# Rearranging the joins between stages: query groups, guess groups, last heads' values, a row sum in its PSUM copy and a shorter Newton step

## The chip, the core and the metric

The kernel runs on one core of one Trainium2 chip. The time is device microseconds of one execution; lower is better. In the profile PE is TensorE's matmul side, PEld its weight loads, DVE is VectorE, ACT is ScalarE, POOL is GpSimd and SP is SyncE, which here issues nearly all DMAs.

## The reference

Four layers with residuals on a sequence of 2048 tokens of 640 features, in bf16: spectral layer A, memory layer B, A, B.

```python
def _A_ref(x, w_r, w_i):                      # x is layer-normed
    X = rfft2(x.astype(float32)) * (w_r + 1j * w_i)
    return irfft2(X, s=(2048, 640)).astype(bfloat16)

def _B_ref(x, mem0, Wq, Wk, Wv, Wo, seg_len): # 64 segments of 32 tokens, 8 memory rows, 32 heads of 128
    mem = mem0
    for s in range(64):
        h = concat([mem, x[segment s]])
        q, k, v = h @ Wq, h @ Wk, h @ Wv
        p = softmax(where(mask, q @ k.T * 128 ** -0.5, -1e9))
        o = (p @ v) @ Wo
        mem = o[:8]
        out[segment s] = o[8:]

x = x + _A_ref(layernorm(x)); x = x + _B_ref(layernorm(x))
x = x + _A_ref(layernorm(x)); x = x + _B_ref(layernorm(x))
```

## The kernel before

**Layer A** does its Fourier transforms as matmuls against tables. `spectrum` transforms, filters and transforms back along one axis. `tokens` (L567) finishes 16 rows of 128 tokens each: `spectrum_d` and `tokens(s0)` on PE, a PSUM copy of row s0 by ACT into x (L597), then the layer norm of the next layer. The statistics come from DVE (`stats`, L603), only for row 15 from ACT (`act_stats`, L606): an Identity pass with a summed output (L609), a Square pass with a summed output that uses the sum as its bias (L610), and on POOL the mean (L611). `inverse(q)` turns the variance of a pair of rows into a reciprocal square root: Ln and Exp on ACT (L112, L113), then a Newton step in `_ln_inverse`. It has five steps on POOL (L117 to L121) for pairs 0 to 6 and four on DVE (L115, L119 to L121) for the last pair, 7. `norm(q)` scales the pair's rows on DVE (L127) and stores them to `xn`.

Inside the same stage the next layer B is prepared (`BStart`). `add_u` sums the rows of each segment on PE (L1541). `rows_in` and `rows_out` transpose the normed rows into `hT`. `guess1` (L1554) multiplies the segment means by Wv for groups of heads given by `GUESS` (L1552), each group in one PSUM bank, and `guess1_out` (L1567) copies each bank to SBUF, the last group by ACT and the one before by DVE. The result, times Wo (`guess2`, L1627), is a guess of each segment's memory row, so that all 64 segments can run at once; a later check compares it with the true memory rows.

**Layer B** (`_b_fast_pass`, L1080) runs over heads h = 0 to 33. Heads 0 and 1 have their queries in `q_x` before and after the guess: four groups of 15 segments (480 columns), one of 3 (96 columns) and a tail of one segment (28 + 4 columns), each a chain of five matmuls into a PSUM tile that ACT copies out with the scale (L1149, L1138). These tiles, the guess's, those of the key and value chains, and in the end those of the wide sums, share a pool of three banks (`pj`). In step h the dense chains of head h (`dense`: keys, queries, values) are interleaved by `merge` with dependent work of earlier heads (`dep`): scores of head h-1, sums of the softmax, and on odd h the `value_group`s of heads h-3 and h-2. `merge` runs, after dense item i, the dependent steps until n * len(dense) reaches (i + 1) * len(dep); `pause` is an empty step. A value group is four matmuls (two for the last) into one of two `pso` banks (L1277), then a product with the reciprocal sums on DVE (L1291 to L1294), which frees the bank. The reciprocals of heads up to 30 come back from DRAM as a broadcast (`sums_back`, L1261).

At h = 32 there are no dense chains left. First come the scores of head 31 beside output matmuls (`begin` makes a list of seven blocks of four matmuls of the output projection, L1470). Then `wide` holds five sums of head 31 (`sums_wide`: four matmuls, then Ln and Exp on ACT, L1267 to L1270), `fill` seven output blocks, and `groups` the five value groups of head 30. In step 33 the value groups of head 31 are merged with a third list of output blocks. `_FastOut.run` then finishes the output projection, and for the first memory layer normalises each finished block of 128 tokens for the second spectral layer.

The order on PE, ACT and DVE is the order of the calls (`manual_schedule`); inside the head loop SP's is too. Around `tokens`, POOL's and SP's orders are the scheduler's.

Of the kernel before, what the change touches and what calls it, by code (L numbers as in the profile page):

```python
# [10 lines left out]
FP32 = mybir.dt.float32  # L11
BF16 = mybir.dt.bfloat16
I32 = mybir.dt.int32
ALU = mybir.AluOpType
# [5 lines left out]
S, D = 2048, 640  # L20
# [87 lines left out]
def _ln_inverse(nc, pool, mv, nt, eps_t, small):  # L108
# [5 lines left out]
    if small is nc.vector:  # L114
        small.scalar_tensor_tensor(out=t, in0=mv[:, :nt, 1], scalar=LN_EPS, in1=r0, op0=ALU.add, op1=ALU.mult)  # L115
    else:
        small.tensor_scalar_add(out=t, in0=mv[:, :nt, 1], scalar1=LN_EPS)  # L117
        small.tensor_tensor(out=t, in0=t, in1=r0, op=ALU.mult)
# [73 lines left out]
class LayerA:  # L192
# [374 lines left out]
    def tokens(self, x_dst, xn_dst, handoff=None):  # L567
# [16 lines left out]

        def tokens(s0):
# [11 lines left out]
            nc.scalar.copy(out=halves(x[:, s0, :]), in_=psy[:, :, 0:320])  # L597
# [8 lines left out]
        def act_stats(s0):  # L606
            m, scr = mv[s0 // 2][:, s0 % 2, :], Gs[1].rearrange("p a b -> p (a b)")[:, 0:D]
            nm = wk.tile([128, 1], FP32, name="lnnm", tag="lnnm")
            nc.scalar.activation(out=scr, in_=x[:, s0, :], func=ACTF.Identity, scale=-D ** -1.5, accum_out=nm[:])  # L609
            nc.scalar.activation(out=scr, in_=x[:, s0, :], func=ACTF.Square, scale=D ** -0.5, bias=nm[:, 0:1], accum_out=m[:, 1:2])  # L610
            nc.gpsimd.tensor_scalar_mul(out=m[:, 0:1], in0=nm[:], scalar1=-D ** 0.5)  # L611
# [468 lines left out]
def _b_fast_pass(tc, g, bs, env, flag_col, nxt=None):  # L1080
# [29 lines left out]
    if True:  # L1110
# [25 lines left out]
        def q_tail(QT, ps, lo, src0, n):  # L1136
            b = st.qbase(NSEG - 1) + lo
            nc.scalar.mul(out=QT[:, b:b + n], in_=ps[:, src0:src0 + n], mul=scale)  # L1138

        def q_x(w, h):  # L1140
            QT = QTs[h % 2]
            for g_ in range(NG):
# [7 lines left out]
            ps = pj.tile([128, 512], FP32, name="psq", tag="pj")  # L1150
            b = st.kbase(NSEG - 1) + 1
            chain(w["Wq"], h % 2, ps[:, 0:SEG - st.TAIL], hT, b, b + SEG - st.TAIL)
            chain(w["Wq"], h % 2, ps[:, SEG - st.TAIL:SEG], hT, st.TAILK, st.TAILK + st.TAIL)
            q_tail(QT, ps, 0, 0, SEG)
# [182 lines left out]
        if True:  # L1337
            for h in range(H + 2):
# [39 lines left out]
                if h < H:  # L1378
# [4 lines left out]
                    else:  # L1383
# [7 lines left out]
                        else:  # L1391
                            dep = [pause]
# [7 lines left out]
                elif h == H:  # L1400
# [13 lines left out]
                    for i, f in enumerate(wide):  # L1414
                        f()
                        for _ in range(2):
                            (fill or groups).pop(0)()
                    groups.pop(0)()
# [94 lines left out]
class BStart:  # L1513
# [38 lines left out]
    GUESS = ((0, 8), (8, 16), (16, 24), (24, 28), (28, 32))  # L1552
# [246 lines left out]
```

## Time and profile before

| | |
|---|---|
| median of 4 runs | 1563.13 us (1562.32 to 1564.14) |
| profiled execution | 1564.03 us, of which span 1562.2 us |
| PE busy | 1532.5 us, 98% of the span, 14482 matmuls |
| DVE, ACT, POOL busy | 809.5, 772.9, 234.8 us |
| granted TensorE clock | 0.999 |

Busy times are summed over the span. A row of the timeline is start, duration, engine, line, operation, tiles and count, and in brackets the idle time just before it and what ended it. The two pairs of layers are alike: the join from A to B is at 104 to 124 us and again at 872 to 892, the end of the last head at 612 to 656 and at 1378 to 1422. Matmul ends are modelled: two matmuls of one stream overlap in the records, and a pause is read best from one matmul's start to the next one's.

### The profile page before, as it was taken

Reading aid. Unit: us, or ns where it says so; the run is one execution under the profiler, and the core shown is the slowest. Engines: PE = TensorE matmul, PEld = TensorE weight load, DVE = VectorE, ACT = ScalarE, POOL = GpSimd, SP = SyncE. Lnnn points to the kernel's source line nnn. Section 1 sums busy time; section 2 is a strip of 40 time slices with the busy share of each in tenths; the row PEclk is TensorE's granted clock in tenths of the full one; section 3 lists DMA queues with packets and bytes.
Section 4 is the critical chain, followed back from the end, with each engine's and each line's share of the span. In section 5 each row is a group of like instructions: output and inputs, shape, how many; then the busy total and the mean of one; then the engine's idle time right before and its main releaser. Section 6 shows DMA issues by size and latency. Waiting matters only on the chain. (4 is left out here: it accounts for less than half of the span.)

```text
span 1562.2 us, 36535 instructions
## 1 busy us (share of the span) xinstructions
PE 1532.5 (98%) x14482; PEld 1077.6 (69%) x14483; DVE 809.5 (52%) x2432; ACT 772.9 (49%) x2251; POOL 234.8 (15%) x327
## 2 busy tenths in 40 slices
PE   7999999999999999999999999999999999999998
PEld 6776666666666666677777766666666666667775
DVE  7873545555456555633367535565455545553111
ACT  4583565556555565511136655556555565562000
POOL 3520121111111121100034101112111121110000
PEclk9999999999999999999999999999999999999999
DMA  4780344334433444646114514344434434327242
GB/s 171 227 298 28 110 142 148 136 126 147 152 138 137 146 127 149 193 107 183 51 48 159 182 49 144 137 138 134 166 126 139 151 122 174 124 99 230 70 128 64
DMA packets 159765, 214.87 MB, mean 138 GB/s; under 512 B 7136, under 2 KB 133096, under 8 KB 151648
## 3 DMA queue, kind: packets, MB, share of 16 engines
q1 hardware_dynamic: 159008, 210.14, 41.0%
q8 instruction: 115, 1.88, 0.5%
q0 software_dynamic: 576, 2.30, 0.4%
q14 instruction: 66, 0.54, 0.1%
HBM read 167.32 MB, written 45.10 MB: 136 GB/s over the span
## 5 line engine op out<-in xcount | busy, mean ns | idle before, releaser
L1128 PEld LDWEIGHTS <-bB_S 128*128 128x128 bf16 x3180 | 261.2, 97 | 179.8 <-issue 0.6
L1187 DVE CAST bB_S<-psk 128x495 bf16<-128x495 f32 (+3 forms) x320 | 191.6, 599 | 277.3 <-PE psk L1128 272.6
L1470 PE MATMUL psx<-Wo_sb,bB_S 128*128 128x320 bf16 x2048 | 287.7, 299 | 0.1
L1207 ACT ACTIVATE bB_S<-pss 128x269 bf16<-128x269 f32 (+5 forms) x576 | 208.8, 386 | 139.0 <-PE pss L1204 138.7
L1470 PEld LDWEIGHTS <-bB_S 128*128 128x128 bf16 x2048 | 197.1, 98 | 74.4 <-DVE bB_S L1291 0.7
L1172 ACT ACTIVATE bB_S<-psq 128x96 bf16<-128x96 f32 x300 | 152.4, 508 | 173.4 <-PE psq L1128 173.4
L1247 POOL TENSOR_TENSOR bB_S<-bB_S,bB_S 128x535 f32<-128x535 f32 x90 | 111.7, 1254 | 821.1 <-DVE bB_S L1239 763.1
L1291 DVE TENSOR_TENSOR bB_S<-pso,bB_S 128x480 bf16<-128x480 f32 (+1 forms) x320 | 192.8, 603 | 78.9 <-DMA bB_S<-Rd 50.4
L1208 DVE TENSOR_TENSOR bB_S<-bB_S,maskf 128x269 bf16<-128x269 bf16 (+5 forms) x576 | 159.0, 289 | 109.2 <-ACT bB_S L1207 109.2
L1196 ACT CAST bB_S<-psv 128x512 bf16<-128x512 f32 (+1 forms) x288 | 162.7, 565 | 80.9 <-PE psv L1194 80.9
L1194 PE MATMUL psv<-bB_S,B2hT_S 128*128 128x256 bf16 x1360 | 168.8, 272 | 0.0
L1194 PE MATMUL psv<-bB_S,B1hT_S 128*128 128x256 bf16 x1360 | 168.7, 272 | 0.0
L1128 PE MATMUL psk<-B2hT_S,bB_S 128*128 128x495 bf16 (+3 forms) x800 | 164.2, 343 | 0.2 <-ACT bB_S L1149 0.2
L1128 PE MATMUL psk<-B1hT_S,bB_S 128*128 128x495 bf16 (+3 forms) x800 | 164.2, 343 | 0.2 <-ACT bB_S L1149 0.2
L1128 PE MATMUL psq<-B2hT_S,bB_S 128*128 128x495 bf16 (+5 forms) x780 | 156.0, 336 | 0.0
L1128 PE MATMUL psq<-B1hT_S,bB_S 128*128 128x495 bf16 (+5 forms) x780 | 155.9, 336 | 0.0
L1194 PEld LDWEIGHTS <-B1hT_S 128*128 128x128 bf16 x1360 | 129.8, 98 | 24.4
L1194 PEld LDWEIGHTS <-B2hT_S 128*128 128x128 bf16 x1360 | 129.8, 98 | 24.4
L1204 PE MATMUL pss<-bB_S 128*128 128x132 bf16 (+8 forms) x1152 | 137.5, 219 | 0.0
L1204 PEld LDWEIGHTS <-bB_S 128*128 128x128 bf16 x1152 | 95.5, 97 | 55.3
L1277 PE MATMUL pso<-bB_S,bB_S 128*128 128x132 bf16 (+8 forms) x1152 | 118.5, 219 | 3.5 <-DVE oTmf L1294 2.8
L1277 PEld LDWEIGHTS <-bB_S 128*128 128x128 bf16 x1152 | 89.1, 98 | 36.3 <-DVE oTmf L1294 4.6
(293 smaller groups left out, 1427.0 us busy)
## 6 DMA issues: line engine op xcount, KB each, us to landing
bB_S<-Rd SPq DMA_DIRECT2D x62, 1070.0 KB
oTx_d<-bB_S SPq DMA_DIRECT2D x60, 512.0 KB
bB_S<-oTx_d SPq DMA_DIRECT2D x46, 512.0 KB
bB_S<-in_B_Wq_dram SPq DMA_DIRECT2D x32, 320.0 KB
bB_S<-in_B_Wk_dram SPq DMA_DIRECT2D x32, 320.0 KB
bB_S<-in_B_Wv_dram SPq DMA_DIRECT2D x32, 320.0 KB
Wo_sb<-in_B_Wo_dram SPq DMA_DIRECT2D x4, 1280.0 KB
B1wv_S<-in_B_Wv_dram SPq DMA_DIRECT2D x10, 512.0 KB
```

The source lines that it names most:

```text
L1128: nc.tensor.matmul(ps, lhsT=w[:, ch, hh * 128:(hh + 1) * 128], rhs=src[:, ch, lo:hi], start=(ch == 0), stop=(ch == 4))
L1172: nc.scalar.mul(out=qv[:, :, 0:SEG], in_=x_view(ps, o, n)[:, :, 1:SW], mul=scale)
L1187: nc.vector.tensor_copy(out=KTs[h % 2][:, lo:hi], in_=ps[:, 0:hi - lo])
L1194: nc.tensor.matmul(ps[:, i * 256:(i + 1) * 256], lhsT=hT[:, ch, st.hcol((t + i) * 128):st.hcol((t + i) * 128) + 128], rhs=w["Wv"][:, ch, : ...
L1196: nc.scalar.copy(out=V[:, t:t + n, :].rearrange("p a b -> p (a b)"), in_=ps[:, 0:n * 256])
L1204: nc.tensor.matmul(ps[:, off - o0:off - o0 + hi - lo], lhsT=KT[:, t * 128:(t + 1) * 128], rhs=QT[:, lo:hi], start=True, stop=True)
L1207: nc.scalar.activation(out=E[:, 0:n], in_=ps[:, 0:n], func=ACTF.Exp)
L1208: nc.vector.tensor_tensor(out=P[:, o0:o0 + n], in0=E[:, 0:n], in1=bs.mask[:, o0:o0 + n], op=ALU.mult)
L1247: nc.gpsimd.tensor_tensor(out=acc, in0=acc, in1=part, op=ALU.add)
L1277: nc.tensor.matmul(pso[:, lo - q0:hi - q0], lhsT=V[:, t, (h % 2) * 128:(h % 2 + 1) * 128], rhs=P[:, off:off + hi - lo], start=(i == 0), st ...
L1291: nc.vector.tensor_tensor(out=oT.rearrange("p (r s j) -> p r s j", r=16, j=2)[:, :, s0:s0 + ns, :], in0=byclass(po), in1=rx, op=ALU.mult)
L1470: self.tc.nc.tensor.matmul(ps[:, 0:320], lhsT=lhs(h, k // 2), rhs=self.g["Wo_sb"][:, h, c0:c0 + 320], start=(h == 0), stop=(h == H - 1))
```

## The change

- `_ln_inverse` on DVE has three steps in place of four; POOL's form stays.
- Row 15's copy out of PSUM also gives the row's sum; the Identity pass of `act_stats` becomes a scaling of that sum.
- `q_x` does the tail and the group of three segments first, then the four groups of 15.
- Head 31's list of dependent steps has one more `pause` in front.
- At h = 32, `wide`, the output blocks and the value groups of head 30 alternate in another order: sums group, (from the third on a value group of head 30 ahead of it), one output block; then the fourth value group, the two blocks left over, the sums, and the last group.
- The last two guess groups have 6 and 2 heads in place of 4 and 4.

```diff
--- before.py
+++ after.py
@@ -113,6 +113,9 @@
     nc.scalar.activation(out=r0, in_=r0, func=ACTF.Exp, scale=-0.5)
     if small is nc.vector:
         small.scalar_tensor_tensor(out=t, in0=mv[:, :nt, 1], scalar=LN_EPS, in1=r0, op0=ALU.add, op1=ALU.mult)
+        small.scalar_tensor_tensor(out=t, in0=t, scalar=-0.5, in1=r0, op0=ALU.mult, op1=ALU.mult)
+        small.scalar_tensor_tensor(out=t, in0=t, scalar=1.5, in1=r0, op0=ALU.add, op1=ALU.mult)
+        return rs, nb
     else:
         small.tensor_scalar_add(out=t, in0=mv[:, :nt, 1], scalar1=LN_EPS)
         small.tensor_tensor(out=t, in0=t, in1=r0, op=ALU.mult)
@@ -582,6 +585,8 @@
                     nc.tensor.matmul(psg[:, e, 0:NF], lhsT=UT[0:m, ch, e, s0, :], rhs=Gd[0:m, ch, e, :], start=(ch == 0), stop=(ch == 2))
             nc.scalar.copy(out=Gs[s0 % 3], in_=psg[:, :, 0:NF])
 
+        nm = wk.tile([128, 1], FP32, name="lnnm", tag="lnnm")
+
         def tokens(s0):
             q, t = s0 // 2, s0 % 2
             if t == 0:
@@ -594,7 +599,10 @@
             nc.tensor.matmul(psy[:, 0, 0:320], lhsT=Ti[:, s0, 0, :], rhs=G[:, 1, 0:320], start=False, stop=True)
             nc.tensor.matmul(psy[:, 1, 0:320], lhsT=Ti[:, s0, 0, :], rhs=G[:, 0, 320:0:-1], start=False, stop=False)
             nc.tensor.matmul(psy[:, 1, 0:320], lhsT=Ti[:, s0, 1, :], rhs=G[:, 1, 320:0:-1], start=False, stop=True)
-            nc.scalar.copy(out=halves(x[:, s0, :]), in_=psy[:, :, 0:320])
+            if s0 < 15:
+                nc.scalar.copy(out=halves(x[:, s0, :]), in_=psy[:, :, 0:320])
+            else:
+                nc.scalar.activation(out=halves(x[:, s0, :]), in_=psy[:, :, 0:320], func=ACTF.Identity, accum_out=nm[:])
             if t == 1:
                 nc.sync.dma_start(out=xd[:, 2 * q:2 * q + 2, :], in_=x[:, 2 * q:2 * q + 2, :])
 
@@ -605,8 +613,7 @@
 
         def act_stats(s0):
             m, scr = mv[s0 // 2][:, s0 % 2, :], Gs[1].rearrange("p a b -> p (a b)")[:, 0:D]
-            nm = wk.tile([128, 1], FP32, name="lnnm", tag="lnnm")
-            nc.scalar.activation(out=scr, in_=x[:, s0, :], func=ACTF.Identity, scale=-D ** -1.5, accum_out=nm[:])
+            nc.scalar.mul(out=nm[:], in_=nm[:], mul=-D ** -1.5)
             nc.scalar.activation(out=scr, in_=x[:, s0, :], func=ACTF.Square, scale=D ** -0.5, bias=nm[:, 0:1], accum_out=m[:, 1:2])
             nc.gpsimd.tensor_scalar_mul(out=m[:, 0:1], in0=nm[:], scalar1=-D ** 0.5)
 
@@ -1139,7 +1146,12 @@
 
         def q_x(w, h):
             QT = QTs[h % 2]
-            for g_ in range(NG):
+            ps = pj.tile([128, 512], FP32, name="psq", tag="pj")
+            b = st.kbase(NSEG - 1) + 1
+            chain(w["Wq"], h % 2, ps[:, 0:SEG - st.TAIL], hT, b, b + SEG - st.TAIL)
+            chain(w["Wq"], h % 2, ps[:, SEG - st.TAIL:SEG], hT, st.TAILK, st.TAILK + st.TAIL)
+            q_tail(QT, ps, 0, 0, SEG)
+            for g_ in (NG - 1, 0, 1, 2, 3):
                 n = GS if g_ < NG - 1 else 3
                 b = st.hcol(st.kbase(g_ * GS))
                 ps = pj.tile([128, 512], FP32, name="psq", tag="pj")
@@ -1147,11 +1159,6 @@
                     nc.tensor.matmul(ps[:, 0:n * SEG], lhsT=w["Wq"][:, ch, (h % 2) * 128:(h % 2 + 1) * 128], rhs=x_view(hT[:, ch, :], b, n)[:, :, 1:SW],
                                      start=(ch == 0), stop=(ch == 4))
                 nc.scalar.mul(out=x_view(QT, st.qbase(g_ * GS), n)[:, :, 0:SEG], in_=ps[:, 0:n * SEG].rearrange("p (s t) -> p s t", t=SEG), mul=scale)
-            ps = pj.tile([128, 512], FP32, name="psq", tag="pj")
-            b = st.kbase(NSEG - 1) + 1
-            chain(w["Wq"], h % 2, ps[:, 0:SEG - st.TAIL], hT, b, b + SEG - st.TAIL)
-            chain(w["Wq"], h % 2, ps[:, SEG - st.TAIL:SEG], hT, st.TAILK, st.TAILK + st.TAIL)
-            q_tail(QT, ps, 0, 0, SEG)
 
         def q_m(w, h):
             QT = QTs[h % 2]
@@ -1389,7 +1396,7 @@
                             for f, p in zip(v0[1:] + v1, parts):
                                 dep += [p, f]
                         else:
-                            dep = [pause]
+                            dep = [pause, pause]
                             for f, p in zip(v0, parts):
                                 dep += [f, p]
                             dep += parts[5:] + [pause]
@@ -1411,11 +1418,14 @@
                     load_block(2, ((NT, 24), (24, HL)))
                     wide = [lambda g_=g_: sums_wide(P[h - 1], Rb[h - 1], g_) for g_ in range(NG)]
                     fill = begin()
-                    for i, f in enumerate(wide):
+                    for n in range(NG):
+                        if n > 1:
+                            groups.pop(0)()
+                        wide[n]()
+                        fill.pop(0)()
+                    groups.pop(0)()
+                    for f in fill:
                         f()
-                        for _ in range(2):
-                            (fill or groups).pop(0)()
-                    groups.pop(0)()
                     post[0]()
                     tail = begin()
                     for f in groups:
@@ -1549,7 +1559,7 @@
         nc.vector.tensor_copy(out=self.hT[:, :, 0:MEM], in_=psm[:, :, 0:MEM])
         nc.vector.tensor_copy(out=self.gq[:, :, 0:1], in_=psm[:, :, MEM - 1:MEM])
 
-    GUESS = ((0, 8), (8, 16), (16, 24), (24, 28), (28, 32))
+    GUESS = ((0, 8), (8, 16), (16, 24), (24, 30), (30, 32))
 
     def guess1(self, pp, q):
         nc = self.tc.nc
```

## Prediction

> **What bounds the kernel now.** I read the page first, then PE's waits over the whole span, then the timeline at the four joins that the diff touches, and last the order in which each engine's instructions stand in the two programs.
>
> ```profile
> span 1562.2 us, 36535 instructions
> PE 1532.5 (98%) x14482; PEld 1077.6 (69%) x14483; DVE 809.5 (52%) x2432; ACT 772.9 (49%) x2251; POOL 234.8 (15%) x327
> PE ps L324 <- DVE A1xn_S L315: 9.9, 1, 9.9
> PE pso L1277 <- DVE oTmf L1294: 2.8, 5, 0.7
> PE psu L1541 <- DVE A2tok_S L127: 1.2, 2, 0.8
> PE psu L1541 <- DVE A1tok_S L127: 1.2, 2, 0.8
> PE psq L1147 <- issue: 0.9, 1, 0.9
> ...
> PE psg L1631 <- ACT bB_S L1149: 0.4, 2, 0.2
> PE psk L1128 <- ACT bB_S L1149: 0.4, 2, 0.2
> ```
>
> TensorE is busy 98% of the span and the change takes no matmul away: both programs have the same PE rows, partly in another order. So only PE's pauses can be won. The rows are label, total us, times, longest us. The 9.9 us are the start and are not touched; some 6 us after the last matmul are the output's store. What the edits can reach is some 7 us in all, in both layers together (counted below). An idle of 0.21 in these rows is the hole behind a matmul whose modelled end (some 170 ns after its last issue) is counted as busy. Counted from start to start, the matmul at 122.06 is followed at 122.43, 375 ns instead of 26, so such a wait costs 0.35 us. I count from start to start below.
>
> The profiled execution took 1564.03 us, 1.8 around its span of 1562.2. The four timed runs have a median of 1563.13, so it is 0.9 above them. About 0.2% (3.1 us) is what a measurement of this kernel can tell from no change.
>
> **Join 1, spectral layer to memory layer (twice): row 15's sum and three Newton steps.**
>
> ```profile
> 105.33 0.72 ACT L609 ACTIVATE A1tok_S<-A1x_S 128x640 bf16<-128x640 bf16 x1
> 105.57 0.19 POOL L118 TENSOR_TENSOR lnrs<-lnrs,lnnb 128x2 f32<-128x2 f32 x1 [0.57 <-ACT lnnb L113]
> 106.63 0.80 DVE L127 TENSOR_SCALAR A1tok_S<-A1x_S,lnmv,lnrs 128x640 bf16<-128x640 bf16 x2 [0.31 <-POOL lnrs L121]
> 106.68 0.43 POOL L611 TENSOR_SCALAR lnmv<-lnnm 128x1 f32<-128x1 f32 x1
> 107.80 0.16 DVE L115 SCALAR_TENSOR_TENSOR lnrs<-lnmv,lnnb 128x2 f32<-128x2 f32 x1 [0.37 <-ACT lnnb L113]
> 109.10 0.68 PE L1541 MATMUL psu<-sel,A1tok_S 128*128 128x64 bf16 x10 [0.84 <-DVE A1tok_S L127]
> ```
>
> Removed on ACT: the Identity pass L609, 0.72 us. Added: the accumulator's read behind the PSUM copy, and a 128x1 scale. In the trace such a read starts 0.1 before its pass ends and the next independent instruction starts 0.09 after the read, so it delays the queue by 0.12; the nearest row to the scale is L113 (128x2, 0.20 us, dependent start 0.22 later). ACT's Square then starts at 104.89+0.12+0.33+0.11+0.22 = 105.67 instead of 106.24: 0.57 earlier. The bounds of the scale are 0.15 and 0.30. The upper one is the Trainium skill's ("ScalarE: Activation LUTs", Rules for kernel authors: about 0.3 us per ACTIVATE plus 0.83 ns an element). By it the gain on ACT is 0.47 instead of 0.57; the sum is the same, since ACT is not last here. I take the row.
>
> What is last is the pair before. DVE's norm of rows 12-13 (L127 at 106.63) waits for POOL's Newton chain, which waits for L113, now 0.12 later. And POOL's queue changes: in the new order the mean of row 15 (L611) stands behind POOL's first multiply (L118) instead of behind its last step. Its row is 0.43 us, beside a bf16 pass on DVE; the nearest quieter row, L117, is 0.20 to 0.30. It also waits for the new ACT scale (done by 105.65), but that is no further delay, L118 ends at 105.9. So norm(6) starts 0.12 + (0.25 to 0.45) later, about 107.05 to 107.2, lasts 0.80, and DVE is free for L115 at 107.8 to 107.95 where ACT would have allowed 107.25. Newton loses one DVE step, whose start-to-start is 0.195. The last norm thus starts at 108.4 to 108.55 instead of 108.59. PE, 0.4 to 0.6 later from its own first wait, is ready at 108.7 to 108.85, just before. Gain on PE 0.05 to 0.2; without POOL's move it would be 0.5. I take 0.15 each, **0.30**.
>
> The other sites of the shorter Newton (16 rows behind each output block of the first memory layer, 16 x 0.195 = 3.1 us of DVE busy) lie beside PE's output matmuls, with DVE idle over 1 us before each. Only the last row ends near PE's need, at the join to the second spectral layer (L127 ends 793.12, PE's stage-1 matmul starts 793.17 behind work until 793.14): **0.03**.
>
> SP's order changes too: Wk's load is issued behind the last xn store instead of ahead of it, some 1.5 us later. Wk is first read 20 us later, so it costs nothing by itself; it pushes the train of weight loads some 0.5 us later (rival 2).
>
> **Join 2, first query matmul (twice): guess groups 30/2 instead of 28/4.**
>
> ```profile
> 115.98 0.37 ACT L1569 CAST bB_S<-psvb 128x256 bf16<-128x256 f32 x1 [0.58 <-PE psvb L1563]
> 117.65 4.33 PE L1147 MATMUL psq<-B1hT_S,bB_S 128*128 128x480 bf16 x24 [0.89 <-issue]
> ```
>
> The first query matmul starts at 116.40, 0.05 after the last guess copy. With 128 columns instead of 256 that copy takes 0.26 (0.37 and 0.59 for 256 and 512: 0.86 ns a column). DVE's copy grows from 256 to 384 columns (0.42 to 0.56) and starts 0.29 later, ending at 116.25, level with ACT. So 0.10 is won in layer 2. In layer 1 PE then pauses 0.89 us between its first and second query matmul on no semaphore, and a 16384-byte packet of the instruction queue runs just before it (115.16 to 116.35): I read it as instructions arriving late. The Trainium skill ("Runtime: NRT & Kernel Launch", Instruction fetch mechanics) says that crossing a 16 KiB block is mostly hidden. By that rule layer 1 gains its 0.10 like layer 2. By the trace it gains none of it, and the first matmul, which the pause covers, is now 28 columns instead of 480: 0.17 of work comes out from under it. I take the trace: +0.10 - 0.17 = **-0.07** (by the rule +0.20).
>
> **Join 3, short query groups first (two chains in each layer).**
>
> ```profile
> 122.43 1.74 PE L1631 MATMUL psg<-bB_S,Wo_sb 128*128 128x64 bf16 x54 [0.21 <-ACT bB_S L1149]
> ```
>
> Three PSUM buffers rotate. Before, the 480-column group stands three tiles ahead of the guess (and of the first key chain), with only 0.45 us of matmuls between, less than its 0.57 us copy. After, a full group stands between: four waits of 0.35 go, 1.40. New: in the second chain the first full group takes the tail's buffer, two tiles back. The tail's last matmul starts 0.23 after its first, ends 0.16 later, ACT copies 0.04 later for 0.20, PE may go 0.05 later: 0.68. PE has 0.25 + 0.22 of work: a wait of 0.21, twice, 0.42. The copy of the guess by DVE (0.48) is needed one 1.0 us group later and is hidden. Net **+0.98**. Bounds: 0.7 (new waits as long as the old) to 1.40 (none).
>
> **Join 4, values of the last heads (twice).** The extra pause at head 31 does nothing: merge places step n after dense item ceil(...), with 25 steps on 12 items every step after the pauses falls behind the same item as 24 did, and PE's order there is equal. Its wait of 0.6 to 0.7 us stays. At h = 32 the order does change: two value groups move ahead of output blocks.
>
> ```profile
> 639.10 0.31 SPq L1261 DMA_DIRECT2D bB_S<-Rd  x1
> 647.24 0.66 DVE L1291 TENSOR_TENSOR bB_S<-pso,bB_S 128x480 bf16<-128x480 f32 x1 [4.46 <-PE psw L1267]
> 648.10 0.41 PE L1277 MATMUL pso<-bB_S,bB_S 128*128 128x132 bf16 x4 [0.59 <-DVE oTmf L1294]
> 648.75 0.41 PE L1277 MATMUL pso<-bB_S,bB_S 128*128 128x132 bf16 x4 [0.23 <-DVE oTmf L1292]
> ```
>
> Before, the third and fourth group wait for DVE to free one of two buffers: 1.15 us from start to start. After, from 642.03 with 0.245 for a sums or value group and 0.54 for four output matmuls, the groups come up at 643.6, 644.6 and 645.66. But DVE cannot scale the first before the reciprocals are there: the broadcast issued at 639.10 has its 16th completion at 645.81 (1411.92 in layer 2, 3.8 us after the first sums group in both). Then DVE's 0.86 until PE may go: the third group starts at 646.76, a wait of 1.10 in place of 1.15. The sums groups keep up with ACT's Ln (643.2, 644.5, 645.8 against PE's 643.85, 644.9, 646.9). By the whole sequence head 31's first group starts at 650.52 instead of 650.65: 0.13 each, **0.26**.
>
> **Sum.** 0.30 + 0.03 - 0.07 + 0.98 + 0.26 = 1.5 us. 1564.03 - 1.5 = 1562.5 in that execution, 1561.6 at the median: 0.10%, too little to be told from none.
>
> **Rivals.**
> 1. More is won: POOL's move does not delay the pair before (+0.7), layer 1's late instructions come in time (+0.9 and the 0.17), the new waits at the tail do not show (+0.4). All of them give 3.7 us, 1559.4; about two are needed for 3.1. For it: the waits removed are real, 3.4 us a layer in the rows above. Against it: each has something named that is nearly as late.
> 2. The instruction stream starves. The 15 short matmuls of a query chain now follow 200 guess matmuls at 29 ns, or 160 at 30 ns, at four places, and lengthen the fast stretch in which PE eats its instructions; the weight loads, later by SP's move, share the DMA engines. Price: one late block, 0.9 us in the trace, up to the 2.5 from packet start to resumption. Averaged over four places it makes the kernel 0.2% slower from (3.1 + 1.5)/4 = 1.2 us a place; at 1.5 it gives 1566.1. For it: the pause at 117.65. Against: three of the four places show none.
> 3. Nothing moves (the gain is under 0.7 us): 1562.9. Head 31 already is such a no-op.
>
> **How the numbers follow.** Forecast 0.50 (0.02 of it beyond the bound), rival 1 0.30, rival 2 0.15, rival 3 0.05. Faster by over 0.2%: 0.32. Within: 0.48 + 0.05 = 0.53. Slower: 0.15. The range 1558.8 to 1564.6 takes in most of rival 1 and half of the way to rival 2; the forecast's own is 1560.4 to 1562.8.
>
> **What would show it.** Right: psg and psk gone from PE's waits, with two waits of about 0.2 between the first short and the first full query group; L1541's second wait still near 0.8 and its first longer; L1277's waits near 5 and 0.5 us in all, with DVE's first L1291 of head 30 starting at the broadcast's landing. Wrong: L1541's waits at half, or an issue wait of 1 us or more at a short query group.

## The result and the profile after

| | before | changed | compared |
|---|---|---|---|
| median, us | 1563.36 (1561.52 to 1565.62, 60 runs) | 1561.84 (1560.15 to 1563.44, 40 runs) | ratio 0.9991, 95% 0.9986 to 0.9995 |
| profiled execution, us | 1564.03, span 1562.2 | 1562.13, span 1560.3 | clock 0.999 in both |

The change makes the kernel faster by 0.09%, 1.5 us by the medians. That is below the 0.2% that the prediction took as the least that can be told from no change; over this many runs, though, the interval excludes no change. The forecast was 1561.6. The total fits better than its terms do. Two of the terms had the wrong size and one had the wrong sign, and they partly cancel.

From the page of the changed kernel, then its waits of PE (label, total us, times, longest us):

```profile
PE 1532.4 (98%) x14482; PEld 1077.7 (69%) x14483; DVE 807.4 (52%) x2414; ACT 771.9 (49%) x2251; POOL 234.4 (15%) x327
...
PE ps L327 <- DVE A1xn_S L318: 9.6, 1, 9.6
PE pso L1284 <- DVE oTmf L1301: 3.6, 4, 1.1
PE psu L1551 <- DVE A1tok_S L130: 0.9, 2, 0.8
PE psu L1551 <- DVE A2tok_S L130: 0.9, 2, 0.8
PE psq L1135 <- issue: 0.7, 2, 0.3
```

PE's busy time is the same (1532.5 before), so the gain is in pauses, as forecast. The rows of psg (L1631 before) and of the first key group psk (L1128 before) are gone. The sums of each memory join (L1551, L1541 before) wait 0.9 instead of 1.2. There are two waits on no semaphore ("issue") where there was one. And the value groups' row (L1284) has grown from 2.8 to 3.6.

Join 1 in the timeline (start, us, engine, line, output<-inputs, idle before it and its releaser), first the row of before that the prediction does not show, then the changed kernel:

```profile
107.13 0.68 PE L1541 MATMUL psu<-sel,A1tok_S 128*128 128x64 bf16 x10 [0.36 <-DVE A1tok_S L127]
...
105.40 0.20 POOL L121 TENSOR_TENSOR lnrs<-lnrs,lnnb 128x2 f32<-128x2 f32 x1 [0.66 <-ACT lnnm L616]
105.68 0.23 POOL L618 TENSOR_SCALAR lnmv<-lnnm 128x1 f32<-128x1 f32 x1
105.99 0.19 POOL L122 TENSOR_TENSOR lnrs<-lnrs,lnnb 128x2 f32<-128x2 f32 x1
106.76 0.20 ACT L113 ACTIVATE lnnb<-lnnb 128x2 f32<-128x2 f32 x1
106.77 0.80 DVE L130 TENSOR_SCALAR A1tok_S<-A1x_S,lnmv,lnrs 128x640 bf16<-128x640 bf16 x2 [0.71 <-POOL lnrs L124]
107.28 0.68 PE L1551 MATMUL psu<-sel,A1tok_S 128*128 128x64 bf16 x10 [0.77 <-DVE A1tok_S L130]
107.49 0.15 DVE L115 SCALAR_TENSOR_TENSOR lnrs<-lnmv,lnnb 128x2 f32<-128x2 f32 x1
...
108.58 0.68 PE L1551 MATMUL psu<-sel,A1tok_S 128*128 128x64 bf16 x10 [0.18 <-DVE A1tok_S L130]
```

The mean of row 15 (L618) stands in the middle of POOL's Newton chain, as the prediction had it, and takes it from 105.68 to 105.99. ScalarE's Exp for the last rows (L113) is done at 106.96, but VectorE begins L115 only at 107.49, behind the norm that POOL delayed. The first of PE's two waits has grown (0.36 to 0.77) and the second has shrunk (0.84 to 0.18).

Joins 2 and 3, first the guess copies and the first query matmul in a second profile of before, then the changed kernel:

```profile
115.80 0.42 DVE L1569 CAST bB_S<-psvb 128x256 bf16<-128x256 f32 x1 [1.56 <-PE psvb L1563]
116.34 0.10 PEld L1147 LDWEIGHTS <-bB_S 128*128 128x128 bf16 x1
116.38 0.37 ACT L1569 CAST bB_S<-psvb 128x256 bf16<-128x256 f32 x1 [0.58 <-PE psvb L1563]
116.81 2.46 PE L1147 MATMUL psq<-B1hT_S,bB_S 128*128 128x480 bf16 x10 [0.46 <-ACT bB_S L1569]
...
115.17 0.56 DVE L1579 CAST bB_S<-psvb 128x384 bf16<-128x384 f32 x1 [1.87 <-PE psvb L1573]
115.46 0.27 ACT L1579 CAST bB_S<-psvb 128x128 bf16<-128x128 f32 x1 [0.58 <-PE psvb L1573]
115.84 0.13 PEld L1135 LDWEIGHTS <-bB_S 128*128 128x128 bf16 x2 [0.54 <-issue]
115.87 0.17 PE L1135 MATMUL psq<-B1hT_S,bB_S 128*128 128x28 bf16 x1 [0.45 <-DVE bB_S L1579]
116.39 0.37 PE L1135 MATMUL psq<-B1hT_S,bB_S 128*128 128x28 bf16 x9 [0.34 <-issue]
126.10 0.20 ACT L1145 ACTIVATE bB_S<-psq 128x32 bf16<-128x32 f32 x1 [4.33 <-PE psq L1135]
126.34 1.41 PE L1159 MATMUL psq<-B1hT_S,bB_S 128*128 128x480 bf16 x6
882.31 0.28 PE L1135 MATMUL psq<-B2hT_S,bB_S 128*128 128x28 bf16 x5 [0.45 <-DMA bB_S<-in_B_Wk_dram]
882.91 0.28 PE L1135 MATMUL psq<-B2hT_S,bB_S 128*128 128x4 bf16 x5 [0.32 <-issue]
```

Both guess copies now end at 115.73, and PE goes 0.14 later; before, it went 0.05 behind ScalarE's. The rows of the weight load (PEld) show why. PE's first load for the query starts 0.12 behind the end of VectorE's copy (116.22 and 115.73), in both layers of all fourteen profiles, whether that is 0.19 or 0.61 behind the last guess matmul. Before, that load was over long before ScalarE's copy ended, and only the matmul waited. Now the copies end level, and the load stands between VectorE's copy and the matmul, which follows the load by 0.03. It is not that PE follows VectorE late as such: behind other work of VectorE's in the same trace it starts within 0.06 us (L1551 at 107.28 and L1284 at 644.95).

In the second chain the first full group (126.34) starts 0.05 behind the end of the copy of the tail, whose buffer it takes. From the start of the matmul ahead of it that is 0.25 us instead of 0.04. This is the new wait of 0.21; a modelled matmul end covers it, so the list of waits has no row for it. In the first layer the pause on no semaphore stands behind the first query matmul, as before, and in the second there is a new one behind the fifth.

Join 4, first layer, with VectorE's scaling (L1298) and the value groups (L1284):

```profile
642.67 0.40 PE L1284 MATMUL pso<-bB_S,bB_S 128*128 128x132 bf16 x4
644.08 0.66 DVE L1298 TENSOR_TENSOR bB_S<-pso,bB_S 128x480 bf16<-128x480 f32 x1 [3.25 <-DMA bB_S<-Rd]
644.95 0.41 PE L1284 MATMUL pso<-bB_S,bB_S 128*128 128x132 bf16 x4 [1.10 <-DVE oTmf L1301]
```

The mechanism is the predicted one: the two groups come early, VectorE waits for the broadcast, and the third group waits. The times are not. The row's 1.10 is idle time; from start to start the wait is 1.26, where the prediction had 1.10. The first sums group started at 640.08, so VectorE starts 4.00 after it and the third group 4.87.

### The profile page after: what moved, and what is told of

Its sections match the earlier page's. It is cut to its first block, busy times and chain, and to the rows that moved or that the text cites. A ratio compares the mean times of both kernels' runs of the same rounds, so it can differ in the third digit from the quotient of the medians.

```text
span 1560.3 us, 36510 instructions
## 1 busy us (share of the span) xinstructions
PE 1532.4 (98%) x14482; PEld 1077.7 (69%) x14483; DVE 807.4 (52%) x2414; ACT 771.9 (49%) x2251; POOL 234.4 (15%) x327
## 4 chain that ended last, share of the span: by engine, by line
PE 92%; DMA 2%; DVE 2%; ACT 1%; issue 1%; POOL 1%; SPq 0%; DVEq 0%; POOLq 0%; ACTq 0%
PE psv L1201 18%; PE psk L1135 18%; PE psx L1480 17%; PE psq L1135 17%; PE pso L1284 4%; PE pss L1211 4%; PE ab L427 2%; DMA bB_S<-Rd 2%; PE psg L585 1%; PE psl L1238 1%; PE psq L1159 1%; PE X L458 1%; PE psu L519 1%; PE psm L911 1%; PE ps L332 1%
## 5 line engine op out<-in xcount | busy, mean ns | idle before, releaser
L1298 DVE TENSOR_TENSOR bB_S<-pso,bB_S 128x480 bf16<-128x480 f32 (+1 forms) x320 | 192.8, 602 | 77.7 <-DMA bB_S<-Rd 52.7
L1284 PE MATMUL pso<-bB_S,bB_S 128*128 128x132 bf16 (+8 forms) x1152 | 118.7, 219 | 3.7 <-DVE oTmf L1301 3.6
L1284 PEld LDWEIGHTS <-bB_S 128*128 128x128 bf16 x1152 | 89.3, 98 | 37.1 <-DVE oTmf L1301 6.1
```

The lines of the kernel that those rows point to most:

```text
L1284: nc.tensor.matmul(pso[:, lo - q0:hi - q0], lhsT=V[:, t, (h % 2) * 128:(h % 2 + 1) * 128], rhs=P[:, off:off + hi - lo], start=(i == 0), st ...
L1298: nc.vector.tensor_tensor(out=oT.rearrange("p (r s j) -> p r s j", r=16, j=2)[:, :, s0:s0 + ns, :], in0=byclass(po), in1=rx, op=ALU.mult)
```

## A ledger of the pauses, and what one execution can tell

The stages are compared by the start of the same PE matmul in two traces. The shift between a matmul ahead of a join and one behind it is what the join gained (negative) or lost. All values are us against the first profile of before, worked out from the matmul starts. Two numbers are layers 1 and 2. Rest is all else: the start, and the value groups that wait for a broadcast in the loop over the heads.

| kernel (one profile each) | join 1 | joins 2, 3: layer 1 | layer 2 | h = 32 | to second spectral layer | rest | all |
|---|---|---|---|---|---|---|---|
| before, again | 0.00, 0.00 | -0.82 | 0.00 | 0.01, -0.01 | 0.00 | -0.25 | -1.08 |
| Newton alone | -0.21, -0.22 | -0.82 | 0.00 | 0.00, -0.02 | -0.05 | 0.22 | -1.11 |
| guess groups alone | 0.01, 0.00 | -0.95 | -0.01 | 0.01, 0.00 | 0.01 | -0.38 | -1.31 |
| query order alone | 0.01, 0.00 | -1.41 | -0.44 | 0.00, -0.02 | 0.00 | 0.62 | -1.25 |
| changed | -0.25, -0.26 | -1.05 | -0.02 | 0.12, 0.04 | -0.04 | -0.36 | -1.83 |
| changed, mean on ScalarE | -0.58, -0.58 | -1.41 | 0.17 | 0.09, -0.01 | -0.05 | 1.11 | -1.25 |
| changed, PE's stream shifted | -0.26, -0.26 | -1.55 | -0.50 | 0.05, 0.04 | -0.05 | -1.43 | -3.94 |
| changed, full group first | -0.27, -0.26 | -1.69 | -0.71 | 0.06, 0.04 | -0.05 | 1.38 | -1.50 |
| changed, old h = 32 | -0.24, -0.25 | -1.26 | -0.21 | 0.01, -0.01 | -0.05 | 0.84 | -1.18 |
| changed, early broadcast | -0.25, -0.25 | -1.26 | -0.30 | -1.15, -1.19 | -0.05 | 1.13 | -3.30 |
| changed, blocks first at h = 32 | -0.27, -0.26 | -1.32 | -0.45 | -0.64, -0.66 | -0.05 | -0.56 | -4.21 |
| three edits together | -0.58, -0.56 | -1.70 | -0.71 | -0.66, -0.67 | -0.04 | -1.04 | -5.95 |

The columns of join 1 and h = 32 repeat to a few hundredths. The column joins 2, 3 moves by the pauses on no semaphore. The rest goes from -1.43 to 1.38, and what makes it up, the start and four value groups' waits, varies between kernels that are equal there. So a single execution's time says little here, and the experiments are read stage by stage.

The control for this is the second profile of before.

> The kernel before, unchanged, profiled a second time. Theory 1: of the differences between the two profiles, the start (TensorE's first wait 9.9 and 9.6 us), the value groups' waits for a broadcast at h = 3 to 31 (0.68 us at 334.6) and the size of the first layer's pause (1.05 us start to start) come with the execution: they differ here from the first profile by 0.2 us or more, while both waits at each memory join (0.53 and 1.01), the four of 0.37 at the guess and the first key group, and h = 32 (0.75 and 0.40) repeat within 0.03. Theory 2: all of these repeat within 0.05 and the differences are the change's doing.

Measured: 1562.44 us, span 1560.7. Theory 1 holds for what it says to repeat. PE's waits at L1541 are 1.2 in all again, and the first group of head 30 waits as before. Of what it says to vary, the first layer's pause did (1.05 beyond the first matmul's own 0.21, now 0.22), the wait of 0.68 is absent (its matmul starts at 335.61 in the first profile, not at 334.6), and the first wait repeated (9.9).

```profile
PE ps L324 <- DVE A1xn_S L315: 9.9, 1, 9.9
PE pso L1277 <- DVE oTmf L1294: 2.3, 4, 0.8
PE psu L1541 <- DVE A2tok_S L127: 1.2, 2, 0.8
```

PE has no row "issue" in this profile: the pause of 0.89 us on which the prediction built its term for join 2 was the longest of all profiles taken.

## The experiments

### Join 1: Newton alone, and the mean off POOL

```diff
 (before)
     if small is nc.vector:
         small.scalar_tensor_tensor(out=t, in0=mv[:, :nt, 1], scalar=LN_EPS, in1=r0, op0=ALU.add, op1=ALU.mult)
+        small.scalar_tensor_tensor(out=t, in0=t, scalar=-0.5, in1=r0, op0=ALU.mult, op1=ALU.mult)
+        small.scalar_tensor_tensor(out=t, in0=t, scalar=1.5, in1=r0, op0=ALU.add, op1=ALU.mult)
+        return rs, nb
```

> The kernel before with the three-step Newton chain on VectorE alone; row 15's sum and POOL's mean stay as they were. Theory 1 (the prediction's term): the last norm of each join waits for VectorE's chain, so one step of 0.195 us goes from the second wait of the memory sums matmul at each join, 0.39 us over both, and 0.03 at the join to the second spectral layer. Theory 2: what the changed kernel won at this join (0.56 us over both) came from the row sum only; then the chain's step lies beside other work and each join gains under 0.05.

Measured: 0.21 and 0.22 at the two joins, 0.05 at the join to the second spectral layer. The second wait of the sums, 0.84 before, is 0.63:

```profile
109.99 0.68 PE L1544 MATMUL psu<-sel,A1tok_S 128*128 128x64 bf16 x10 [0.63 <-DVE A1tok_S L130]
```

Theory 1 holds, and the step of 0.195 is worth itself. The changed kernel has 0.25 and 0.26 there, so its new row sum and the moved mean together bring only 0.04 a join.

```diff
 (changed kernel)
-            nc.gpsimd.tensor_scalar_mul(out=m[:, 0:1], in0=nm[:], scalar1=-D ** 0.5)
...
             inverse(7, nc.vector)
+            nc.scalar.mul(out=mv[7][:, 1, 0:1], in_=nm[:], mul=-D ** 0.5)
```

> The changed kernel with row 15's mean (128x1) computed on ScalarE behind the Exp of the last row pair instead of on POOL in the midst of the Newton chain of the pair before. Theory 1 (POOL's queue, as predicted): in the changed kernel POOL's mean takes the chain of rows 12-13 from 105.68 to 105.99, so the norm of that pair and with it both waits of the memory sums matmul come 0.31 us earlier at each join, 0.6 us over both. Theory 2: another wait comes next, the last pair's Exp on ScalarE (ready at 106.96 in the changed kernel, with VectorE busy until 107.48): then the first wait shortens by 0.3 and the second gives part of it back, under 0.15 us a join. Theory 3: POOL's mean costs nothing, 0.

Measured: 0.58 at each join, 0.32 to 0.33 more than the changed kernel. POOL's chain and what follows, from this kernel's timeline:

```profile
107.10 0.19 POOL L121 TENSOR_TENSOR lnrs<-lnrs,lnnb 128x2 f32<-128x2 f32 x1 [0.66 <-ACT lnnm L616]
107.38 0.20 POOL L122 TENSOR_TENSOR lnrs<-lnrs,lnnb 128x2 f32<-128x2 f32 x1
...
108.47 0.20 ACT L113 ACTIVATE lnnb<-lnnb 128x2 f32<-128x2 f32 x1
108.67 0.67 PE L1551 MATMUL psu<-sel,A1tok_S 128*128 128x64 bf16 x10 [0.45 <-DVE A1tok_S L130]
108.88 0.15 DVE L115 SCALAR_TENSOR_TENSOR lnrs<-lnmv,lnnb 128x2 f32<-128x2 f32 x1
```

From L121 to L122 it is 0.27 here and 0.59 in the changed kernel. The 0.31 of POOL's mean arrives in full at PE: theory 1. Theory 2 is nearly reached: VectorE starts L115 0.21 behind the end of ScalarE's Exp (108.67). In before it followed that Exp by 0.04, so a still faster POOL would gain no more than 0.17. A detail on releasers: L121 is put down to ScalarE's scale L616 here too, though nothing on POOL reads the scale's output any more. It starts 0.15 behind the Exp (106.75 to 106.95) that it does read.

### Joins 2 and 3: guess groups, query order, instruction blocks

```diff
 (before)
-    GUESS = ((0, 8), (8, 16), (16, 24), (24, 28), (28, 32))
+    GUESS = ((0, 8), (8, 16), (16, 24), (24, 30), (30, 32))
```

> The kernel before with guess groups 30/2 instead of 28/4. Theory 1 (VectorE's copy is last): the first query matmul waits for VectorE's copy of 384 columns instead of ScalarE's of 256, and comes 0.01 to 0.02 us earlier after the last guess matmul (0.64 instead of 0.65 start to start); no pause in the second layer, as four full matmuls cover it; in the first layer a pause of 0.23 to 1.05 us as in the two profiles of before. Theory 2 (the prediction): 0.10 us earlier at the first query matmul. Theory 3: the pause in the second layer appears here.

Measured: from the last guess matmul to the first query matmul 0.643 and 0.645 us instead of 0.653 and 0.654, a gain of 0.01. Theory 1 holds in size, though VectorE's copy is not later than ScalarE's: both end at 116.49, and the weight load (116.61) and the matmul (116.64) follow as in the changed kernel. There is no pause in the second layer.

The query order alone, in the kernel before, is the q_x of the diff and nothing else.

> The kernel before with the short query groups first in each query chain; guess groups and the rest as before. Theory 1 (as in the changed kernel): the four waits of 0.37 us ahead of the guess and the first key group go, one of 0.21 comes at each second chain; counted from start to start, TensorE is 0.48 earlier behind the first key group in each layer, and the pause behind the fifth matmul appears in the second layer (0.2 to 0.7 us), which it never did with the full group first: the order alone makes it. Theory 2: the pause in the second layer comes from the guess groups 30/2 (200 matmuls of 29 ns and less cover ahead of it); here it is absent.

Measured: the four waits of 0.37 are gone, one of 0.25 start to start is there in each second chain, and in the second layer this brings 0.44. The pause in the second layer is only 0.04 in this profile, so theory 1's claim that the order alone makes it was not borne out at that size; theory 2's is not shown either, as the pause goes from 0.05 to 0.67 in the changed kernel and its variants.

```diff
 (changed kernel, ahead of layer A1's first matmul; lead is a PSUM tile that nothing reads)
+            for _ in range(108):
+                nc.tensor.matmul(lead[:, 0:16], lhsT=self.g["ones"][:], rhs=self.g["ones"][:, 0:16], start=True, stop=True)
```

> The changed kernel with 108 matmuls of 16 columns on a constant tile ahead of TensorE's first real one, inside the 9.6 us in which it waits for the input: every later TensorE instruction stands 216 places further on in its stream (a matmul and its weight load are two), the rest is unchanged. Theory 1 (instruction blocks): the pauses in the first query chain stand where TensorE passes from one 16384-byte packet of instructions to the next; if a packet holds 256 instructions the place moves 40 instructions on, into the full groups with 0.2 us a matmul, and the pauses behind the first (layer 1) and the fifth matmul (layer 2) fall under 0.15 us: 0 to 0.5 and 0.2 to 0.67 us won. Theory 2: the pause belongs to the place (PSUM handed over, the loads of weights at that time): it stays within 0.2 to 0.67 us behind the same matmuls. Theory 3: it turns up at another place with the same size, and nothing is won.

Measured: both pauses are gone. The 108 matmuls end inside the wait for the input; the ten short matmuls of the first chain go without a break (first layer shown, the second is alike):

```profile
1.14 3.05 PE L287 MATMUL lead<-ones 128*128 128x16 bf16 x108 [1.14 <-DVE ones L1697]
9.70 0.81 PE L333 MATMUL ps<-A1xn_S,A1x_S 128*128 128x128 bf16 x5 [5.51 <-DVE A1xn_S L324]
...
116.01 0.39 PE L1141 MATMUL psq<-B1hT_S,bB_S 128*128 128x28 bf16 x10 [0.45 <-DMA bB_S<-in_B_Wk_dram]
```

Joins 2 and 3 gain 1.55 in layer 1 and 0.50 in layer 2: to 0.01 what the waits and the pause of before (1.05) amount to. It is one profile, and the second layer's pause was down to 0.05 us in others. But none of the six other profiles with the short groups first is free of it in either layer. The 16384-byte packets of the instruction queue bear on the reading. There are 115 of them in the trace of before, one for every 252 of PE's matmuls and weight loads. PE paused over 0.1 us at this place in fourteen first chains, and it resumed 1.26 to 1.92 us behind the end of a packet. Six of them:

| kernel, layer | packet ends | PE resumes | between |
|---|---|---|---|
| before, 1 | 116.36 | 117.65 | 1.30 |
| before again, 1 | 115.83 | 117.24 | 1.41 |
| changed, 1 | 115.13 | 116.39 | 1.26 |
| changed, 2 | 881.58 | 882.91 | 1.32 |
| mean on ScalarE, 2 | 881.73 | 883.22 | 1.49 |
| old h = 32, 1 | 115.85 | 117.75 | 1.90 |

The shift shows that the place is fixed by the position in the stream of instructions. Theory 2 (the place itself) is against it; theory 3 (the same pause elsewhere) did not occur. That the instructions come late is the reading of this, and not shown: four chains with a pause of 0.05 to 0.07 us at the same place resumed 1.27 to 2.17 us behind a packet, so the interval alone does not tell when PE pauses. What sets the size stays open.

```diff
 (changed kernel, q_x: g_ == NG stands for the tail's two chains)
-            for g_ in (NG - 1, 0, 1, 2, 3):          # behind the tail
+            for g_ in (0, NG, 1, NG - 1, 2, 3):
```

> The changed kernel with each query chain in the order full group, tail, full, short group of three, full, full, instead of tail, short, four full. Theory 1 (buffers and late instructions): no group takes a PSUM buffer less than one full group (1.0 us) after its last use, so the two new waits of 0.21 us at the second chain go, 0.42; the pause of 0.21 to 0.67 us that every kernel with the short chain first shows in the second layer behind its fifth matmul goes too, since four of 0.2 us stand ahead of that place; in the first layer the pause starts behind a matmul of 0.2 us instead of 0.01, 0.17 less. Together 0.6 to 1.2 us faster than the changed kernel. Theory 2: the second full group now takes the guess's buffer, whose copy is VectorE's 0.49 us: a wait of 0.2 to 0.4 at each second chain takes the place of the one removed, and only the pause's share is won. Theory 3: the second layer's pause stays, as its instructions are the ones that are late and not the matmuls that are short.

Measured: 0.64 in layer 1 and 0.69 in layer 2 against the changed kernel, 1.33 in all. PE's rows, the first of the first chain and those of the second:

```profile
116.69 1.27 PE L1161 MATMUL psq<-B1hT_S,bB_S 128*128 128x480 bf16 x5 [0.45 <-DMA bB_S<-in_B_Wk_dram]
...
126.05 1.21 PE L1161 MATMUL psq<-B1hT_S,bB_S 128*128 128x480 bf16 x5
127.09 0.40 PE L1135 MATMUL psq<-B1hT_S,bB_S 128*128 128x28 bf16 x10
127.35 1.63 PE L1161 MATMUL psq<-B1hT_S,bB_S 128*128 128x480 bf16 x11
```

No row waits behind the first. The 0.21 of each second chain is won exactly, so theory 1 holds in its mechanism and theory 2's wait for the guess's buffer did not come. The sum is over theory 1's 0.6 to 1.2. The rest are the pauses of the one profile of the changed kernel (0.50 and 0.48 us), here 0.07 and none.

### Join 4: old order, early broadcast, output blocks first

> The changed kernel with the order of stage h = 32 put back to that of before; all else as changed. Theory 1 (read from the two traces): the new order costs 0.10 us in the first memory layer and 0.05 in the second, so head 31's first value group comes 0.05 to 0.10 earlier, counted from the first sums group (8.62 us after it, where the changed kernel has 8.72). Theory 2 (the prediction): the new order is worth 0.13 us a layer, and this kernel loses that. Theory 3: both orders wait for the same landing, and the difference is chance: it is not repeated.

Measured: 0.01 and -0.01 against before, where four profiles with the new order have 0.05 to 0.12 in layer 1 and -0.01 to 0.04 in layer 2. Theory 1 in layer 1: the new order loses 0.05 to 0.12 there. In layer 2 it loses at most 0.04, hardly more than the scatter. Theory 2, the prediction's 0.13 of gain, falls.

```diff
 (changed kernel)
-            if h % 2 or h == H - 2:
-                for a in range(h if h == H - 2 else h - 1, h + 1):
+            if h % 2:
+                for a in range(h - 1, h + 1):
...
+                        if h == H - 1:
+                            v0[4] = lambda f=v0[4]: (f(), nc.sync.dma_start(out=Rbs2[0], in_=Rd[H - 3][0:1, :].to_broadcast([128, 4 * NR])))
```

> The changed kernel with the broadcast for head 30 taken from the reciprocals of head 29 and issued at h = 31 behind head 28's last value group, some 10 us earlier; head 30 is then scaled by head 29's reciprocals. The order of all engines is kept. Theory 1: the landing of head 30's broadcast, 3.8 us after the first sums group, sets the third value group; with the data there early its wait of 1.22 to 1.27 us (start to start) goes to under 0.25, and PE is about 1.0 us earlier in each layer. Theory 2: VectorE's scaling (0.86 us a group) is as much the limit as the landing: at least 0.6 us of wait remain. Theory 3: the wait turns up at the sums groups of PE, behind ScalarE's Ln and Exp of the group before; PE then gains under 0.4 us a layer.

Measured: h = 32 is 1.27 and 1.23 shorter than in the changed kernel. The third group (644.81) waits for nothing, and VectorE scales right behind PE:

```profile
643.22 0.66 DVE L1298 TENSOR_TENSOR bB_S<-pso,bB_S 128x480 bf16<-128x480 f32 x1 [1.27 <-PE pso L1284]
644.81 0.40 PE L1284 MATMUL pso<-bB_S,bB_S 128*128 128x132 bf16 x4
```

The landing is the cause of the third group's whole wait (theory 1). This kernel leaves out head 30's own reciprocals, so it measures the wait and cannot be used. As long as those land no earlier, what is left is to give PE other work for these 1.2 us a layer.

```diff
 (changed kernel, h = 32)
-                    for n in range(NG):
-                        if n > 1:
-                            groups.pop(0)()
-                        wide[n]()
-                        fill.pop(0)()
-                    groups.pop(0)()
-                    for f in fill:
-                        f()
+                    for n in range(2):
+                        wide[n]()
+                        fill.pop(0)()
+                    groups.pop(0)()
+                    for n in range(2, NG):
+                        wide[n]()
+                        fill.pop(0)()
+                        if n == 3:
+                            groups.pop(0)()
+                    for f in fill:
+                        f()
+                    groups.pop(0)()
```

> The changed kernel with another order at h = 32: one value group behind the second sums group, one behind the fourth, and all seven output blocks ahead of the third value group, so that only three value groups of head 30 stand ahead of the sums of head 31 and two behind. Theory 1: the landing of head 30's broadcast sets when the third group can go (4.87 us after the first sums group); in this order it comes up at about 5.5, the wait of 1.22 to 1.27 us goes, and PE is 1.1 to 1.3 us earlier in each layer. Theory 2: VectorE starts its scaling no earlier, so the fourth and fifth group, behind the sums, wait for it instead: 0.5 us or more of the wait comes back there. Theory 3: the sums groups, now closer to one another in the row, wait for ScalarE's Ln and Exp: over 0.3 us.

Measured: 0.76 and 0.70 shorter than the changed kernel. The third group waits for nothing, but the first output block that needs head 31 does:

```profile
644.82 0.40 PE L1284 MATMUL pso<-bB_S,bB_S 128*128 128x132 bf16 x4
...
652.23 0.16 DVE L1299 TENSOR_TENSOR oTmf<-pso,bB_S 128x4 bf16<-128x4 f32 x1
652.37 1.80 PE L1484 MATMUL psx<-Wo_sb,bB_S 128*128 128x320 bf16 x12 [0.57 <-DVE bB_S L1298]
```

Theory 2 named this kind of loss (0.5 comes back) but looked for it at the fourth and fifth group. It comes later: VectorE's chain for head 31 takes 0.97 a full group and ends at 652.39, and some 0.5 of the 1.25 are given back there.

### The three edits together

> The changed kernel with three of the experiments' edits together: row 15's mean on ScalarE instead of POOL, each query chain in the order full, tail, full, short, full, full, and at h = 32 all seven output blocks ahead of the third value group. Theory 1 (they lie at different places and add): 0.65 us from the mean (0.29 and 0.36), 0.4 from the two waits of 0.21 and 0 to 0.8 from the late instructions, and 1.5 from h = 32 (0.75 a layer, since VectorE's scaling gives 0.5 of the 1.25 back at the first block that needs head 31): 2.6 to 3.3 us under the changed kernel, 1558.5 to 1559.3 us, ratio to the kernel before 0.997. Theory 2: the joins feed one another (work that comes earlier meets transfers that do not): under 1.5 us, ratio over 0.998.

Measured: 1558.75 us median (1557.57 to 1559.67, 6 runs) against 1563.40 for before (11 runs), ratio 0.9970, 95% 0.9958 to 0.9982. That is 3.1 us under the changed kernel's median. Theory 1 holds: the gains add, and the ledger has each at its place. It is faster than both kernels: its slowest run is below the fastest of the changed kernel (1560.15).

The same with the two PSUM pools exchanged, to see what the 0.64 ahead of the first query matmul waits for:

> As the kernel with the three edits together, with the two PSUM pools of the memory layer's pass allocated in the other order, so that the first query group lies in other banks than the last guess groups. All engines' orders are equal. Theory 1 (the wait of 0.64 us, start to start, ahead of the first query matmul is for the banks that the guess copies leave): it falls under 0.2 us in each layer, up to 0.9 us won over both, unless the instructions behind it are late. Theory 2: the wait is for the whole pool of the stage before, whatever the bank, or for the hidden rows that ScalarE and VectorE copy: it stays at 0.64 and the time is that of the other kernel within 0.1%.

Measured: 1558.25 us (1558.05 to 1559.65), ratio 0.9968 (0.9956 to 0.9980), and 0.643 us start to start in both layers. Theory 2: the banks are not the cause. Whether PE waits for VectorE because of the whole pool or of the hidden rows stays open.

## Why the prediction was right, and where its steps were not

The total was right (1.5 us forecast, 1.52 by the medians, 0.8 to 2.2 by the interval), and so was the case: nearly nothing, since each removed wait has something nearly as late behind it. Added up from the ledger the change is worth 0.51 + 0.05 - 0.21 + 0.97 - 0.11 = 1.2 us, within that interval. That the medians meet the forecast to 0.02 us is luck: two of the five terms came out as forecast, and the others were off by +0.21, -0.14 and -0.37. Term by term:

- **Join 1, forecast 0.30, measured 0.51.** The mechanism held, with POOL's mean in the chain of the pair before. Counted from row 15's last matmul, the norm of rows 12-13 starts 0.41 us later, inside the forecast 0.37 to 0.57. The gain is larger by 0.10 a join because four small terms were each put 0.02 to 0.03 too long: ScalarE's delay by the accumulator's read (0.09, not 0.12), POOL's mean (0.31, where a gain of 0.15 implies some 0.34), VectorE's time from that norm to L115 (0.72, not 0.75, as VectorE takes up L115 before the norm's recorded end), and from there to the last norm (0.58, not 0.60). "Without POOL's move it would be 0.5" came out as 0.58. The sign named for this join, a second wait of L1541 still near 0.8, does not follow from the prediction's own times, which leave about 0.2; measured 0.18. ScalarE's new scale (L616) took 0.19, as the row taken for it. The Trainium skill's 0.3 ("ScalarE: Activation LUTs", Rules for kernel authors) is stated for an ACTIVATE with a [128,1] bias operand, and L616 has none.
- **Join to the second spectral layer, forecast 0.03, measured 0.04 to 0.05.** Right.
- **Join 2, forecast -0.07, measured about -0.21.** Two steps failed. The 0.10 of the smaller copy was 0.01: the prediction saw that VectorE's copy would end level with ScalarE's, but not that PE's weight load stands behind VectorE's copy, so that the matmul comes 0.14 after it and not 0.05. And the pause was taken for a fixed feature of the first layer. It varies from 0.11 to 1.05 there in the four profiles with the old query order (mean 0.40), and from 0.13 to 0.49 in the changed kernel and the four variants that leave this place alone (mean 0.29). In the second layer it is new: 0.05 to 0.67 in these five (mean 0.34), because 0.1 us of short matmuls stand ahead of it instead of 0.8 us of full ones. With these means the term is 0.02 + 0.11 - 0.34 = -0.21. They are means of few profiles: without the 1.05 of the first one the old order's mean is 0.18, this term -0.43, and all five add up to 1.0 us. The Trainium skill says that the crossing of a 16 KiB block is mostly hidden ("Runtime: NRT & Kernel Launch", Instruction fetch mechanics), by which the prediction's other sum was +0.20. If the pauses are late instructions, up to 1.05 us was not hidden at this place; for all 115 packets in the trace of before, PE's waits have one row on no semaphore.
- **Join 3, forecast 0.98, measured 0.97** from start to start: four waits of 0.35 gone, two of 0.21 in their place. Right, and both were worked out from the order of buffers and three durations.
- **Join 4, forecast 0.26, measured -0.11** (the mean of the four profiles with the new order). The mechanism was right (the third group waits for the broadcast; head 31's pause a no-op: PE's order there is equal). The sum of times was not. VectorE's start was put 3.87 behind the first sums group, 0.09 behind the landing, and comes at 4.00, so in the first layer the third group comes at 4.87 instead of 4.73, and its wait is 1.26 and not 1.10. Then PE has a hole of 0.10 ahead of head 31's sums, in the old order too, that the step did not count. Against a gain of 0.13 these are everything. The old order lost the same landing in two waits, so there was little to gain from moving two groups ahead of it. The sign of 5 and 0.5 us for L1277's waits did not come either: they are 3.6 us in one row.

Rival 2, a starving instruction stream, was the right worry at the wrong price, if that is what the pauses are: up to 0.67 us at one of the four places and not 1.2 at each. Of rival 1's three parts, the pause in layer 1 is chance, and POOL's move does delay and the new waits do show; only experiments that change the kernel further won them. Two figures of rival 2 are slips that change no reading here: 160 guess matmuls stand ahead of each chain, not 200, and four places at 1.5 us above 1561.6 would give 1567.6, not 1566.1.

## What to carry to other kernels

When a join is moved, work out what is late next, and size a transfer's landing from the event that starts it: the early groups of join 4 met the same broadcast, and work that does not depend on it had to be put there instead. A small operation on an idle engine is not free if its queue is someone's critical chain: 0.31 us of POOL took most of the 0.37 that the removal of a 0.72 us pass on ScalarE could bring (0.58 without POOL's mean, less the 0.21 of the Newton step). Before a copy is called hidden because it ends level with another, look at what waits for each: a weight load behind the one made 0.09 of 0.10 vanish. And profile the kernel before twice, since a pause that comes and goes with the execution should enter a sum as a mean, not as the value of one trace.

## What the runs showed of the hardware that was not expected

At one place in the first query chain, behind 160 guess matmuls of about 30 ns each, TensorE paused on no semaphore for up to 1.05 us. The pause is bound to a position in the stream of instructions: with 216 more instructions ahead it was gone in both layers. In the second layer none of the seven profiles with four matmuls of 0.2 us ahead of the place has it. VectorE took up its work 0.19 us behind a broadcast's 16th completion in the first memory layer (643.89 in the changed kernel's trace) and 0.12 in the second. And a matmul came 0.05 us behind the copy that it waited for when its weights were loaded already, but 0.14 behind when the load waited for the copy as well.
